# Local attention and a gated feed-forward on one core: source order on every engine in the pairs of blocks too

## The chip, the cores and the metric

The kernel runs on one core of one Trainium2 chip. The metric is the device time of one execution in microseconds (us), the median of several runs.

## The reference

```
q, k, v: (8, 8, 576, 64)   chunks of 64 rows
attn = softmax(q_c k_c^T / 8) per chunk;  out = attn v_c
x = out as (4608 tokens, 512)
h = x @ w_in (512 x 2048);  g = h * clip(h + 3, 0, 6) / 6
y = g @ w_out (2048 x 512)
```

Everything is float32. The kernel gets that precision from matmuls in fp32r: each operand is split into a high half (a cast) and a low half (the operand minus its high half), and three matmuls (high x high, high x low, low x high; L229 to L231, the helper `passes`) make one product.

## The kernel before, in words

The 4608 tokens are nine blocks of 512. Everything is transposed: a block's x and g lie with features on the 128 partitions and 512 tokens in a row. Blocks 0 to 2 are computed plainly (`mm1`, `gate`, `mm2`); beside them the attention of the next blocks runs, and the weights are converted and combined for what follows. Blocks 3 to 8 are three pairs (s = 0, 1, 2). For a pair, each of the two products of 2 x 2 blocks of matrices is done with seven products instead of eight, numbered 1 to 7, whose sums and differences are made on DVE and POOL.

A pair has 112 slots, each of six matmuls on PE. The first 56 are `first_product`: 8 columns p of 7 slots, in the order `ORDER_A` = 1, 5, 6, 7, 2, 3, 4. The products 1, 5 and 7 of a column take one of four PSUM banks `acc`, 6 one of two banks `h`; 2, 3 and 4 add on to the banks of 1, 5 and 7. What follows each product is put into a table `todo` by slot, and `tick(slot)` at the slot's end writes it out: after 1 a copy p1 (ACT, L612); after 6 the additions u2 = product 6 + p1 and u4 = product 5 + u2 (DVE, L575); after 7 the sum h = product 7 + u4; then for h, 2, 3 and 4 a ReLU on ACT (L586) and the gate on DVE (L587), for 3 and 4 with an addition of u2 before it. The gates fill tiles g0 to g3 (`gs`), each for two columns. After the gate of 3, POOL makes two differences (L595), into g and into t20 to t23.

The second 56 slots are `second_product`: in the order `ORDER_B` = 1, 5, 6, 7, 2, 4, 3, for each product 8 slots, two to an operand. The operands are made by `units`, 28 of them, four (for g0 to g3) to a product: a split, which is a cast on ACT (L423) and a subtraction on DVE (L424) into one of 8 buffers `xop`. After the split for product 5, DVE also makes a difference in g (L642); after that for product 6 (from t20 to t23), POOL makes one (L644). They are put into the table from five slots before the second product, one each 1.75 slots. The operands of the next pair's first product come from `x_operands`: seven splits, with four differences between them (L435, on POOL), put at slots 100 to 112.

Beside the first two pairs runs the attention of the next pair, four units of it, at slots 6, 23, 40 and 78: scores on PE (64 matmuls, L150), their maximum m, the difference e and then exp (L165, L169, ACT L170), the sum z and its reciprocal (L175 to L177), e times that (L179), eight transposes on PE (L188) and a copy (L190), 64 values matmuls (L200) and a copy (L211). Weights come in 1 MB tiles `ws` through SP (`fetch`, L418, three buffers), as do qk and v (L132, L142).

The order on each engine's queue is what the change is about. Up to the end of block 2 the program stands within `tc.manual_schedule()`, entered at line 281 and held by `order`: every engine runs its instructions in the order in which the source makes them. `order.close()` at line 559 ends this; from there a list scheduler of the framework orders each engine's instructions by its own estimate of when they can start, and the order of `todo` only guides it.

Of the kernel before, what the change touches and what calls it, by code (L numbers as in the profile page):

```python
# [42 lines left out]
def tile_kernel(ctx: ExitStack, tc: tile.TileContext, qk_in, v_in, weights, out):  # L43
# [236 lines left out]
    order = ExitStack()  # L280
# [275 lines left out]
        mm2(*item)  # L556
    for _ in made:
        pass
    order.close()
    std.close()  # L560
    op = pool("op2", 2)
    gs = pool("gs", 1)
# [132 lines left out]
    def tick(slot):  # L695
        for _, f in sorted(todo.pop(slot, []), key=lambda t: t[0]):
            f()
# [24 lines left out]
        second_product(s, base + SLOTS)  # L722
    for slot in sorted(todo):
        tick(slot)


# [24 lines left out]
```

## Time and profile before

| | us |
|---|---|
| median of 3 runs | 829.07 (828.84 to 829.14) |
| the profiled execution | 828.22 |
| its span | 826.4 |
| PE busy | 807.9 (98%) |
| DVE busy | 619.1 (75%) |
| ACT busy | 365.2 (44%) |
| POOL busy | 138.5 (17%) |

The first pair's first matmul starts about 328 us after the span's start, the second pair's at 497.4, the third's at 667.4. The granted TensorE clock is full throughout. Rows of a timeline give start, length, engine, line and operation, the tile written and those read, shapes, and in brackets how long the engine had been idle and what ended that. PE is the tensor engine's matmuls, PEld its weight loads, DVE the vector engine, ACT the scalar engine, POOL GpSimd, SP the queue of the DMAs. Consecutive alike instructions share a row (x4), with their time from first start to last end.

### The profile page before, as it was taken

How to read it: one execution, taken by the hardware profiler on the slowest of the kernel's cores; microseconds unless marked ns; L12 is line 12 of the kernel's file. 1: busy time of each engine (PE TensorE's matmuls, PEld its weight loads, DVE VectorE, ACT ScalarE, POOL GpSimd, SP SyncE). 2: the span in 40 equal slices, each digit the busy share in tenths (PEclk: the TensorE clock that was granted, in tenths of full speed). 3: DMA queues.
4: the chain of work that ended last, by engine and by line, in shares of the span. 5: the costliest groups of instructions: out<-in, count | busy, mean ns of one | idle time of the engine just before them, and what ended most of it. 6: DMA issues, size and time to landing. Idle time of an engine off the chain costs nothing.

```text
span 826.4 us, 13753 instructions
## 1 busy us (share of the span) xinstructions
PE 807.9 (98%) x5714; PEld 653.3 (79%) x5714; DVE 619.1 (75%) x760; ACT 365.2 (44%) x459; POOL 138.5 (17%) x79
## 2 busy tenths in 40 slices
PE   8989999999999999999999999999999999999998
PEld 5767788888877888788788887888788887878886
DVE  5888765887868864777889666777898566679951
ACT  4767752434335453433463432434644423336330
POOL 1300000000000000122262031222450212227100
PEclk9999999999999999999999999999999999999999
DMA  8982002669877971565645777567455664555573
GB/s 341 403 352 78 1 1 77 210 224 283 256 252 252 319 284 52 192 230 205 247 184 207 238 255 241 187 224 255 178 204 182 226 230 178 181 204 187 192 229 127
DMA packets 50413, 172.85 MB, mean 209 GB/s; under 512 B 4656, under 2 KB 16944, under 8 KB 39728
## 3 DMA queue, kind: packets, MB, share of 16 engines
q1 hardware_dynamic: 50352, 171.99, 59.4%
q8 instruction: 45, 0.74, 0.4%
q14 instruction: 16, 0.13, 0.0%
HBM read 133.17 MB, written 38.80 MB: 208 GB/s over the span
## 4 chain that ended last, share of the span: by engine, by line
PE 75%; DVE 14%; ACT 5%; issue 3%; DMA 1%; POOL 1%; SPq 0%; ACTq 0%; DVEq 0%; POOLq 0%
PE acc L229 16%; PE acc L230 15%; PE acc L231 15%; PE h L229 8%; PE h L230 7%; PE h L231 7%; PE two L200 2%; DVE xop L424 2%; PE two L188 2%; DVE u L107 1%; DVE g L587 1%; DVE u L575 1%; PE two L150 1%; DMA w<-w_in_out 1%; DVE e L169 1%
## 5 line engine op out<-in xcount | busy, mean ns | idle before, releaser
L229 PE MATMUL acc<-xop,ws 128*128 128x512 f32 x528 | 208.5, 396 | 4.7 <-DVE u L575 4.7
L230 PE MATMUL acc<-xop,ws 128*128 128x512 f32 x528 | 205.7, 390 | 0.0
L231 PE MATMUL acc<-xop,ws 128*128 128x512 f32 x528 | 205.3, 390 | 0.0
L229 PEld LDWEIGHTS acc<-xop,ws 128*128 128x128 f32 x528 | 99.1, 188 | 28.0 <-DVE u L575 7.1
L424 DVE TENSOR_TENSOR xop<-g,xop 128x1024 fp32r<-128x1024 f32 x72 | 103.3, 1468 | 21.5 <-ACT xop L423 21.5
L595 POOL TENSOR_TENSOR g<-g 128x512 f32<-128x512 f32 x24 | 34.7, 1446 | 500.4 <-DVE g L587 500.4
L231 PEld LDWEIGHTS acc<-xop,ws 128*128 128x128 f32 x528 | 99.1, 188 | 21.1
L230 PEld LDWEIGHTS acc<-xop,ws 128*128 128x128 f32 x528 | 99.2, 188 | 19.7
L423 ACT CAST xop<-g 128x1024 fp32r<-128x1024 f32 x72 | 74.3, 1050 | 78.8 <-PE acc L231 51.3
L229 PE MATMUL acc<-g,w 128*128 128x512 f32 x192 | 76.5, 399 | 0.5 <-ACT g L249 0.5
L229 PE MATMUL h<-x,w 128*128 128x512 f32 x188 | 75.1, 400 | 0.9 <-ACT w L112 0.9
L231 PE MATMUL h<-x,w 128*128 128x512 f32 x188 | 74.1, 394 | 1.7 <-POOL w L114 1.1
L230 PE MATMUL acc<-g,w 128*128 128x512 f32 x192 | 75.4, 393 | 0.2 <-DVE g L251 0.2
L231 PE MATMUL acc<-g,w 128*128 128x512 f32 x192 | 75.4, 393 | 0.0
L230 PE MATMUL h<-x,w 128*128 128x512 f32 x188 | 73.8, 392 | 0.0
L586 ACT ACTIVATE r<-acc,half 128x512 f32<-128x512 f32 x72 | 48.6, 686 | 26.8 <-DVE acc L575 26.0
L586 ACT ACTIVATE r<-h,half 128x512 f32<-128x512 f32 x24 | 16.5, 687 | 95.2 <-DVE h L575 95.2
L246 DVE SCALAR_TENSOR_TENSOR r<-r,h 128x512 f32<-128x512 f32 x48 | 32.7, 682 | 33.6 <-ACT r L245 33.5
L230 PE MATMUL h<-xop,ws 128*128 128x512 f32 x144 | 56.1, 390 | 0.1
L229 PE MATMUL h<-xop,ws 128*128 128x512 f32 x144 | 56.3, 391 | 0.0
L231 PE MATMUL h<-xop,ws 128*128 128x512 f32 x144 | 56.1, 389 | 0.0
L587 DVE SCALAR_TENSOR_TENSOR g<-r,acc 128x512 f32<-128x512 f32 x72 | 48.6, 682 | 7.3 <-ACT r L586 7.1
(90 smaller groups left out, 1255.4 us busy)
## 6 DMA issues: line engine op xcount, KB each, us to landing
ws<-b SPq DMA_DIRECT2D x42, 1024.0 KB, 4.8
ws<-a SPq DMA_DIRECT2D x24, 1024.0 KB, 4.9
ws<-a SPq DMA_DIRECT2D x24, 768.0 KB, 4.3
w<-w_in_out SPq DMA_DIRECT2D x16, 1024.0 KB, 14.8
qk<-qk_in SPq DMA_DIRECT2D x16, 1024.0 KB, 6.1
v<-v_in SPq DMA_DIRECT2D x17, 512.0 KB, 5.2
out_t<-o SPq DMA_DIRECT2D x32, 256.0 KB, 4.7
a<-hl SPq DMA_DIRECT2D x32, 256.0 KB, 3.3
```

The lines of the kernel that those rows point to most:

```text
L107: DVE.tensor_tensor(out=u, in0=u, in1=r, op=ALU.add)
L188: PE.transpose(out=self.tp[:, a, i], in_=self.e[:, a, 2 * i:2 * i + 2].rearrange("p c t -> p (c t)"), identity=ident)
L200: PE.matmul(self.po[o, s, a, i, :], lhsT=self.v[rows, a, i, o], rhs=self.aT[rows, a, i, o], start=True, stop=True)
L229: PE.matmul(ps, lhsT=a_h, rhs=b_h, start=first, stop=False, skip_group_check=more)
L230: PE.matmul(ps, lhsT=a_h, rhs=b_l, start=False, stop=False, skip_group_check=more)
L231: PE.matmul(ps, lhsT=a_l, rhs=b_h, start=False, stop=last, skip_group_check=more)
L246: DVE.scalar_tensor_tensor(out=r, in0=r, scalar=1.0, in1=h, op0=ALU.min, op1=ALU.mult)
L423: ACT.copy(out=t[:, :, 0], in_=src)
L424: DVE.tensor_tensor(out=t[:, :, 1], in0=src, in1=t[:, :, 0].bitcast(F32), op=ALU.subtract)
L586: return (lambda: ACT.activation(out=r, in_=ps, func=AF.Relu, bias=half, scale=1.0 / 6.0), lambda: DVE.scalar_tensor_tensor(out=out, in0=r ...
L587: lambda: DVE.scalar_tensor_tensor(out=out, in0=r, scalar=1.0, in1=ps, op0=ALU.min, op1=ALU.mult))
L595: sub = lambda o, x, y: lambda: POOL.tensor_tensor(out=o, in0=x, in1=y, op=ALU.subtract)
```

## The change

`order.close()` moves from line 559, behind block 2, to the end of the function: the pairs stand within the manual schedule as well. No instruction is added or taken out; each engine's order in the pairs becomes that of the source. From line 560 on the changed kernel's lines have numbers one lower (L586 for L587, L641 for L642); the texts use those of before.

```diff
@@ -556,7 +556,6 @@
         mm2(*item)
     for _ in made:
         pass
-    order.close()
     std.close()
     op = pool("op2", 2)
@@ -722,6 +721,7 @@
         second_product(s, base + SLOTS)
     for slot in sorted(todo):
         tick(slot)
+    order.close()
```

Three places on DVE follow, all in the first pair; the second has the same.

First, the change of columns p = 0 to p = 1, with the first attention unit beside it. Before:

```order
L587 SCALAR_TENSOR_TENSOR g0_3238<-r_3300,acc_3256 128x512
L587 SCALAR_TENSOR_TENSOR g0_3238<-r_3312,acc_3273 128x512
L165 TENSOR_REDUCE m_3363<-two_3317 128x16
L169 TENSOR_TENSOR e_3374<-two_3317,m_3363 128x1024
L175 TENSOR_REDUCE z_3441<-e_3374 128x16
L575 TENSOR_TENSOR u2_3384<-h_3377,p1_3357 128x512
```

Now:

```order
L586 SCALAR_TENSOR_TENSOR g0_3237<-r_3299,acc_3255 128x512
L574 TENSOR_TENSOR acc_3272<-acc_3272,u2_3270 128x512
L165 TENSOR_REDUCE m_3362<-two_3316 128x16
L586 SCALAR_TENSOR_TENSOR g0_3237<-r_3311,acc_3272 128x512
L169 TENSOR_TENSOR e_3373<-two_3316,m_3362 128x1024
L574 TENSOR_TENSOR u2_3383<-h_3376,p1_3356 128x512
```

The sum z has gone from ahead of u2 to seven instructions behind u4, and the addition for product 4 stands behind the gate of product 3.

Second, the last column of the first product, p = 7, around u2, u4 and h. Before:

```order
L424 TENSOR_TENSOR xop_4027<-g1_3239,xop_4027 128x2x512
L424 TENSOR_TENSOR xop_4059<-g2_3240,xop_4059 128x2x512
L575 TENSOR_TENSOR u2_4010<-h_4003,p1_3987 128x512
L642 TENSOR_TENSOR g1_3239<-t21_3243,g1_3239 128x1024
L575 TENSOR_TENSOR u4_4011<-acc_3994,u2_4010 128x512
L642 TENSOR_TENSOR g2_3240<-t22_3244,g2_3240 128x1024
L575 TENSOR_TENSOR h_4003<-acc_4015,u4_4011 128x512
```

Now:

```order
L424 TENSOR_TENSOR xop_4011<-g0_3237,xop_4011 128x2x512
L574 TENSOR_TENSOR u2_4009<-h_4002,p1_3986 128x512
L574 TENSOR_TENSOR u4_4010<-acc_3993,u2_4009 128x512
L424 TENSOR_TENSOR xop_4026<-g1_3238,xop_4026 128x2x512
L574 TENSOR_TENSOR h_4002<-acc_4014,u4_4010 128x512
L586 SCALAR_TENSOR_TENSOR g3_3240<-r_4023,h_4002 128x512
L586 SCALAR_TENSOR_TENSOR g3_3240<-r_4045,acc_3979 128x512
L424 TENSOR_TENSOR xop_4058<-g2_3239,xop_4058 128x2x512
```

The two differences L642 have left this place; the split of g0 for product 1, which with the L642 of g0 stood in columns 1 and 2 before, has come to it, and the split of g2 stands behind two gates.

Third, the operands of products 5 and 6 at the start of the second product. Before:

```order
L424 TENSOR_TENSOR xop_4121<-g3_3241,xop_4121 128x2x512
L587 SCALAR_TENSOR_TENSOR g3_3241<-r_4070,acc_4015 128x512
L642 TENSOR_TENSOR g3_3241<-t23_3245,g3_3241 128x1024
L424 TENSOR_TENSOR xop_4137<-g0_3238,xop_4137 128x2x512
L424 TENSOR_TENSOR xop_4149<-g1_3239,xop_4149 128x2x512
L424 TENSOR_TENSOR xop_4165<-g2_3240,xop_4165 128x2x512
L424 TENSOR_TENSOR xop_4185<-g3_3241,xop_4185 128x2x512
L424 TENSOR_TENSOR xop_4205<-t20_3242,xop_4205 128x2x512
```

Now:

```order
L424 TENSOR_TENSOR xop_4120<-g3_3240,xop_4120 128x2x512
L586 SCALAR_TENSOR_TENSOR g3_3240<-r_4069,acc_4014 128x512
L424 TENSOR_TENSOR xop_4136<-g0_3237,xop_4136 128x2x512
L641 TENSOR_TENSOR g0_3237<-t20_3241,g0_3237 128x1024
L424 TENSOR_TENSOR xop_4148<-g1_3238,xop_4148 128x2x512
L641 TENSOR_TENSOR g1_3238<-t21_3242,g1_3238 128x1024
L424 TENSOR_TENSOR xop_4164<-g2_3239,xop_4164 128x2x512
L641 TENSOR_TENSOR g2_3239<-t22_3243,g2_3239 128x1024
L424 TENSOR_TENSOR xop_4184<-g3_3240,xop_4184 128x2x512
L641 TENSOR_TENSOR g3_3240<-t23_3244,g3_3240 128x1024
L424 TENSOR_TENSOR xop_4204<-t20_3241,xop_4204 128x2x512
```

All four differences stand here now, each behind its own split for product 5. On POOL the first L435 has gone from ahead of the four L644 to behind them. On PE a few single matmuls of the first product move by some places, and the values matmuls of the third attention unit, which stood in three pieces in each of the two pairs that have one, are one piece. On SP the loads of qk and v have moved against those of the weights and the outputs; the first qk of a pair is now loaded when the pair begins, where it was loaded some tens of slots earlier.

## The prediction

> **What bounds the kernel now.** I read the page's busy times first, then the waits of PE from 325 us on (where the pairs begin), then the timeline around each wait.
>
> ```profile
> PE 807.9 (98%) x5714; PEld 653.3 (79%) x5714; DVE 619.1 (75%) x760; ACT 365.2 (44%) x459; POOL 138.5 (17%) x79
> PE acc L229 <- DVE u L575: 4.7, 6, 1.5
> 692.96 0.39 PE L231 MATMUL acc<-xop,ws 128*128 128x512 f32 x1
> 694.22 0.50 PE L229 MATMUL acc<-xop,ws 128*128 128x512 f32 x1 [0.87 <-DVE u L575]
> 694.56 0.39 PE L230 MATMUL acc<-xop,ws 128*128 128x512 f32 x1
> 428.56 0.39 PE L229 MATMUL acc<-xop,ws 128*128 128x512 f32 x1
> 434.00 0.39 PE L229 MATMUL acc<-xop,ws 128*128 128x512 f32 x1
> 767.54 0.39 PE L229 MATMUL h<-xop,ws 128*128 128x512 f32 x1
> 768.07 0.50 PE L230 MATMUL h<-xop,ws 128*128 128x512 f32 x1
> 768.07 0.19 PEld L230 LDWEIGHTS h<-xop,ws 128*128 128x128 f32 x1 [0.56 <-DVE xop L424]
> ```
>
> PE is the bound. Four slots (24 matmuls) go from 428.56 to 434.00, so a matmul starts every 0.227 us and a slot takes 1.36, though a row shows 0.39: an idle of PE costs its length plus 0.16. In the pairs PE has six listed waits, all for u4 (L575, which reads the bank that i=3 accumulates on): 4.7 + 6 x 0.16 = 5.7 us. After a wait the next matmul comes 0.34 later instead of 0.23 (694.22 to 694.56), 0.11 more; four of the six are such plain waits (two come right behind values matmuls, which pay it anyway): 0.4. A seventh, unlisted one stands at 768.07: PE reaches slot 72 of the third pair, whose second matmul needs the low half of the i=6 operand, 0.3 before DVE has made it (0.4 with the restart). The change can win no more than these and the pieces below; it loses wherever DVE comes later.
>
> **What goes away.**
>
> ```profile
> 345.90 0.50 PE L229 MATMUL acc<-xop,ws 128*128 128x512 f32 x1 [0.24 <-DVE u L575]
> 413.03 0.51 PE L229 MATMUL acc<-xop,ws 128*128 128x512 f32 x1 [1.15 <-DVE u L575]
> 515.47 0.50 PE L229 MATMUL acc<-xop,ws 128*128 128x512 f32 x1 [0.24 <-DVE u L575]
> 744.00 0.50 PE L229 MATMUL acc<-xop,ws 128*128 128x512 f32 x1 [0.74 <-DVE u L575]
> 342.78 0.39 PE L229 MATMUL acc<-xop,ws 128*128 128x512 f32 x1
> 343.31 1.22 DVE L175 TENSOR_REDUCE z<-e 128x16 f32<-128x1024 f32 x1 [1.12 <-ACT e L170]
> 344.44 0.68 DVE L575 TENSOR_TENSOR u<-h,p 128x512 f32<-128x512 f32 x1
> 360.58 0.39 PE L231 MATMUL acc<-xop,ws 128*128 128x512 f32 x1
> 360.89 1.16 PE L200 MATMUL two<-e,v 64*64 64x64 f32 x64
> 361.99 0.50 PE L229 MATMUL acc<-xop,ws 128*128 128x512 f32 x1
> 362.32 0.39 PE L230 MATMUL acc<-xop,ws 128*128 128x512 f32 x1
> ```
>
> The first of these (345.90, in the second pair 515.47): z stands before u2 on DVE and waits 1.12 for the exp. After the change z comes seven instructions behind u4; i=6 ends with slot 9, when slot 10 starts (342.78), so u2 can start near 343.0 and u4 ends by 344.5, while slot 12 could begin at 342.78 + 2 x 1.36 = 345.5: gone. The one at 694.22 goes with the early L642 of g0. Those at 413.03 (twin in the second pair) and 744.00 are u4 behind two L424 and an L642; they change form, below. The values matmuls (L200) of the third attention unit, in three pieces in the first two pairs, become one piece: entering costs 360.89 - 360.58 - 0.23 = 0.08, leaving about 0.1, the restart 0.1, so 0.3 each, four pieces, 1.2. All that can go: 5.7 + 0.4 + 0.4 + 1.2 = 7.7 us.
>
> **Last column of the first product (p=7), third pair.**
>
> ```profile
> 735.03 0.69 ACT L586 ACTIVATE r<-acc,half 128x512 f32<-128x512 f32 x1 [1.45 <-DVE acc L575]
> 402.38 0.39 PE L229 MATMUL acc<-xop,ws 128*128 128x512 f32 x1
> 741.97 0.39 PE L229 MATMUL acc<-xop,ws 128*128 128x512 f32 x1
> L587 DVE SCALAR_TENSOR_TENSOR g<-r,acc 128x512 f32<-128x512 f32 x72 | 48.6, 682 | 7.3 <-ACT r L586 7.1
> L423 ACT CAST xop<-g 128x1024 fp32r<-128x1024 f32 x72 | 74.3, 1050 | 78.8 <-PE acc L231 51.3
> 417.94 1.23 DVE L424 TENSOR_TENSOR xop<-g,xop 128x1024 fp32r<-128x1024 f32 x1
> 405.94 1.30 POOL L595 TENSOR_TENSOR g<-g 128x512 f32<-128x512 f32 x1 [9.23 <-DVE g L587]
> 407.19 3.45 DVE L424 TENSOR_TENSOR xop<-g,xop 128x1024 fp32r<-128x1024 f32 x2 [0.73 <-ACT xop L423]
> 401.34 1.22 DVE L179 TENSOR_TENSOR e<-e,z 128x1024 f32<-128x1024 f32 x1
> ```
>
> DVE's new order, with 0.7 for a gate, an addition or a ReLU: the ReLU of i=3 ends 735.7, gate 736.4, addition for i=4 737.05, its ReLU 737.8, gate 738.55; ACT then copies p1 and casts g0 (1.05) to 739.25, L424 of g0 (1.23) ends 740.5, u2 and u4 741.85. Slot 54, i=3, starts at 741.97: no wait. L424 of g1, now between u4 and h, ends 743.0 and h 743.6; slot 55 (i=4) wants h's bank at 743.33 and waits 0.3. The gate of i=2 ends 745.75, 0.1 late for slot 56. With restarts 0.6.
>
> In the first two pairs z also stands before the gate of i=3. First pair: slot 48 starts at 402.38, the addition for i=3 ends 403.5, z with its two small steps 405.1, the gate 405.75; so POOL's two L595 (1.30 each) begin about 405.8, and L179 falls beside the first. L424 beside an L595 took 3.45 for two where one takes 1.23. L179 never met POOL, so its price lies between 1.22 (alone) and 2.3 (the second of those L424); I take the upper, since it too reads two SBUF tiles. Then u4 ends 411.75, h 413.5, PE waits 0.35 and 0.3, with restarts 0.9 a pair; at 1.22 all comes 0.65 earlier and both waits vanish.
>
> The Trainium skill, SBUF — State Buffer, section "Who interferes with whom", says that a VectorE instruction with two SBUF inputs and a GpSimd one that reads SBUF exclude each other; L179 would then be held, and the sum would have these 0.9 twice; without the rule for L179 it is 1.8 lower. No row of L179 shows it.
>
> **Start of the second product: the large term.** The splits of the i=5 operands (L424 of g0 to g3) are needed one each two slots from slot 64, those of i=6 (L424 of t0 to t3, the tiles t20 to t23) from slot 72.
>
> ```profile
> 425.08 9.04 DVE L424 TENSOR_TENSOR xop<-g,xop 128x1024 fp32r<-128x1024 f32 x4
> 426.37 13.36 POOL L644 TENSOR_TENSOR g<-g,t 128x1024 f32<-128x1024 f32 x4 [2.30 <-DVE xop L424]
> 753.50 13.43 POOL L644 TENSOR_TENSOR g<-g,t 128x1024 f32<-128x1024 f32 x4
> 763.54 3.39 POOL L644 TENSOR_TENSOR g<-g,t 128x1024 f32<-128x1024 f32 x1
> 757.89 3.43 DVE L424 TENSOR_TENSOR xop<-g,xop 128x1024 fp32r<-128x1024 f32 x1
> 761.24 3.42 DVE L642 TENSOR_TENSOR g<-t,g 128x1024 f32<-128x1024 f32 x1
> 764.59 3.42 DVE L424 TENSOR_TENSOR xop<-t,xop 128x1024 fp32r<-128x1024 f32 x1
> ```
>
> While POOL runs L644, every L424 and L642 takes 3.42 instead of 1.23: the two engines alternate, one instruction each, 13.4 / 4 = 3.35 a round, of which DVE works 1.1 and POOL 2.25. Before, a round served one split; against PE's 2.72 for two slots DVE lost 0.6 a round and its lead just sufficed (768.07 is where it didn't). The new order puts L642 of g0 to g3 between the i=5 splits; three of them stood in the first product before. L644 of a block still waits only for the L424 of that block (it overwrites what that split reads), not for L642: the fourth L644 starts at 763.54 while L642 of the same block is still running (761.24 + 3.42). When a split ends, DVE has L642 queued and goes on; POOL gets its turn after it. So a round is split 1.1, L642 1.13, L644 2.25: 4.5 us per two slots.
>
> Third pair, continued: L424 of g2 ends 747.2; addition, ReLU, gate of i=3 749.3; L595 twice to 751.9, L424 of g3 held till then, to 753.0; gate of i=4 753.6; i=5 split of g0 754.75. Slot 56 begins near 745.1, so slot 64 at 756.2: lead 1.65 with the 0.23 of its first matmul. The four rounds end the splits of g1, g2, g3, t0 at 759.2, 763.7, 768.15, 772.65; without waits PE would want t0's at 756.2 + 8 x 1.36 + 0.23 = 767.3. The four waits (0.1, 1.6, 1.6, 1.7) with restarts add up to 5.4. The split of t1 ends 773.8, early again; from there DVE needs 1.13 against 2.72.
>
> First pair, by the same steps: h ends 413.5, the gate of i=2 415.6, L424 of g2 417.15, the gate of i=3 419.3, L595 421.9, L424 of g3 423.0, the gate of i=4 423.6, the i=5 split of g0 424.7; PE has slot 55 from 413.6, the values matmuls from 415.0, slot 56 from 416.25, slot 64 from 427.25 (lead 2.75). t0 ends 424.7 + 4 x 4.48 = 442.6. L435, now behind the L644s on POOL, then takes one more turn (2.2) before t1 ends at 445.95, wanted at 441.1: 4.9. Second pair the same, 4.9.
>
> **Other queues.** On SP the qk loads move later.
>
> ```profile
> DMA to landing us min/median/max: 4.7/6.1/13.2
> 497.42 0.39 PE L229 MATMUL acc<-xop,ws 128*128 128x512 f32 x1
> 497.19 1.28 DVE L656 TENSOR_TENSOR o<-h,u 128x512 f32<-128x512 f32 x2
> ```
>
> The tightest is the second pair's first, now behind the first output of L656: issued near 498.3, wanted by the scores behind slot 6, 497.4 + 9.6 = 507.0; 6.1 lands at 504.4: hidden, and it would cost 4.5 at the worst landing of 13.2. The v loads have over ten slots. ACT's and PE's other moves follow DVE's; the last eight DVE instructions keep their order but for one split, so the tail is unchanged.
>
> **Sum.** Waits after: 4.9 + 4.9 + 5.4 + 0.9 + 0.9 + 0.6 = 17.6; before 7.7; +9.9 us. The profiled execution took 828.22 (span 826.4 and 1.8 around it) and would come to 838.1; the median of the runs shown is 829.07, 0.85 above it, so I say 839.0.
>
> **Rivals.** Faster: the hold does not act on the new order and a round costs DVE only 1.23 + 1.13 = 2.4, under 2.72. Then 15.2 of the 17.6 vanish: 829.1 + 2.4 - 7.7 = 823.8. It decides by the round c: with the first pair's lead no wait arises for 4(c - 2.72) < 2.75, c < 3.4, and the whole breaks even near c = 3.9. For it: rounds of 3.35 caused no wait in two pairs. Against: L642 itself stands at 3.42 beside L644. Half the loss: POOL takes its turn only after L642, so that the next split slips in before L644 (L644 waiting for L642 as well). Then t0 ends 440.3, t1 443.6 in the first pair, 3.3 a pair with restarts: 834. Against it speaks 763.54. No difference: the gains and a loss of about 2.5 a pair cancel; it needs c near 3.9, between the round seen (3.35) and the one worked out (4.5).
>
> **Chances.** The forecast (834.5 to 844) 0.70, half the loss (831.5 to 835) 0.12, faster 0.12, no difference 0.06. A difference under 0.2% can't be told from none here; slower is 0.70 + 0.12 = 0.82. Of the range, 831.5 is the half case with both L179 terms gone, 843.5 the sum with the p=7 terms twice as large and L435 holding t1 in full.
>
> **What would show it.** PE waits for DVE xop L424 of 1 to 2 us at slots 68, 70, 72 and 74, where there are none now; L642 at 1.2 and L644 at about 4.5 apart; no waits near 345.9, 515.5 and 694.2; L200 in runs of 64 only; small waits on u4 and h in p=7. It is wrong if L644 stays 3.35 apart in that stretch or runs clear of the i=5 splits, or if PE waits for scores.

## The result and the profile after

The changed kernel takes 838.45 us (median; 838.17 to 839.65), the kernel before on the same chip 828.96: a ratio of 1.0118, 95% interval 1.0101 to 1.0136. 839.0 had been forecast. The profiled execution is the 839.65 one, span 837.5. 1.56 of that lies ahead of the pairs: PE waits for the first qk load of all (`L150 ... 1.6 <-DMA qk<-qk_in 1.6`), whose place the change does not touch. Lines from L560 on have numbers one lower: L641 is the DVE difference L642, L643 the POOL difference L644, L574 the additions, L586 the gates, L594 the POOL differences L595.

The busy times of the changed kernel, and the waits of PE in its pairs that the view lists, which leaves the shortest out (us in total, times, longest):

```profile
PE 809.2 (97%) x5714; PEld 651.7 (78%) x5714; DVE 621.1 (74%) x760; ACT 364.5 (44%) x459; POOL 135.3 (16%) x79
PE acc L230 <- DVE xop L424: 7.3, 7, 1.5
PE h L230 <- DVE xop L424: 5.0, 5, 1.5
PE acc L229 <- DVE u L574: 0.5, 1, 0.5
```

Busy times hardly tell the two kernels apart (PE 807.9 before, DVE 619.1). The waits do: the six for u4 with 4.7 us have become one of 0.5, and twelve for a split's low half, 12.3 us, have appeared. Where, the timeline of PE in the first pair shows. The four rows without a bracket are the first matmuls of slots 0, 64, 80 and of the next pair; the bracketed ones are the second matmuls of slots 68, 70, 72 and 74:

```profile
329.40 0.39 PE L229 MATMUL acc<-xop,ws 128*128 128x512 f32 x1
428.07 0.39 PE L229 MATMUL acc<-xop,ws 128*128 128x512 f32 x1
434.58 0.50 PE L230 MATMUL acc<-xop,ws 128*128 128x512 f32 x1 [0.68 <-DVE xop L424]
439.04 0.50 PE L230 MATMUL acc<-xop,ws 128*128 128x512 f32 x1 [1.45 <-DVE xop L424]
443.51 0.50 PE L230 MATMUL h<-xop,ws 128*128 128x512 f32 x1 [1.45 <-DVE xop L424]
446.84 0.50 PE L230 MATMUL h<-xop,ws 128*128 128x512 f32 x1 [0.32 <-DVE xop L424]
456.23 0.39 PE L229 MATMUL acc<-xop,ws 128*128 128x512 f32 x1
502.01 0.39 PE L229 MATMUL acc<-xop,ws 128*128 128x512 f32 x1
```

Such starts cut each pair into three stages. Us, first / second / third pair:

| | slots 0 to 64 | 64 to 80 | 80 to the next pair, or the end |
|---|---|---|---|
| before | 100.73 / 101.07 / 89.31 | 23.08 / 23.08 / 22.19 | 45.78 / 45.78 / 47.57 |
| changed | 98.67 / 99.00 / 87.57 | 28.16 / 28.17 / 27.47 | 45.78 / 45.78 / 47.56 |

Slots 0 to 64 gained 5.87 over the three pairs, slots 64 to 80 lost 15.45, the rest stayed: +9.57. The lossy stretch on DVE and POOL, first pair:

```profile
429.96 1.21 DVE L641 TENSOR_TENSOR g<-t,g 128x1024 f32<-128x1024 f32 x1
431.09 3.43 DVE L424 TENSOR_TENSOR xop<-g,xop 128x1024 fp32r<-128x1024 f32 x1
434.45 1.21 DVE L641 TENSOR_TENSOR g<-t,g 128x1024 f32<-128x1024 f32 x1
430.11 3.33 POOL L643 TENSOR_TENSOR g<-g,t 128x1024 f32<-128x1024 f32 x1 [1.16 <-DVE xop L424]
434.60 3.31 POOL L643 TENSOR_TENSOR g<-g,t 128x1024 f32<-128x1024 f32 x1 [1.16 <-DVE xop L424]
```

A round goes from 430.11 to 434.60, 4.49 us. L643 is released by the end of a split and begins with L641, which was queued and goes on undisturbed (1.21); L643 does its own 2.2 only then, and the next split stands from 431.09 until that is over (3.43). PE takes 2.72 for the two slots that one round serves.

One execution of a kernel below, that with L642 ahead of the i=7 splits, took 1339.3 us at a mean granted clock of 0.557; its ratio is of the others, but it is the one that was profiled, so no stages are read from that kernel.

### The profile page after: what moved, and what is told of

Its sections match the earlier page's. It is cut to its first block, busy times and chain, and to the rows that moved or that the text cites. A ratio compares the mean times of both kernels' runs of the same rounds, so it can differ in the third digit from the quotient of the medians.

```text
span 837.5 us, 13780 instructions
## 1 busy us (share of the span) xinstructions
PE 809.2 (97%) x5714; PEld 651.7 (78%) x5714; DVE 621.1 (74%) x760; ACT 364.5 (44%) x459; POOL 135.3 (16%) x79
## 4 chain that ended last, share of the span: by engine, by line
PE 71%; DVE 18%; ACT 5%; issue 4%; DMA 2%; POOL 0%; SPq 0%; DVEq 0%; ACTq 0%; POOLq 0%
PE acc L229 15%; PE acc L230 14%; PE acc L231 14%; PE h L229 7%; PE h L230 7%; PE h L231 7%; DVE xop L424 7%; PE two L200 2%; PE two L150 2%; PE two L188 2%; DVE u L107 1%; DVE g L641 1%; DMA w<-w_in_out 1%; ACT r L585 1%; DVE g L586 1%
## 5 line engine op out<-in xcount | busy, mean ns | idle before, releaser
L424 DVE TENSOR_TENSOR xop<-g,xop 128x1024 fp32r<-128x1024 f32 x72 | 107.7, 1515 | 22.7 <-ACT xop L423 22.7
L594 POOL TENSOR_TENSOR g<-g 128x512 f32<-128x512 f32 x24 | 31.0, 1294 | 501.3 <-PE two L150 297.1
L586 DVE SCALAR_TENSOR_TENSOR g<-r,acc 128x512 f32<-128x512 f32 x72 | 49.0, 681 | 30.8 <-ACT r L585 30.8
L245 ACT ACTIVATE r<-h,half 128x512 f32<-128x512 f32 x48 | 32.8, 683 | 47.9 <-PE h L231 47.9
```

The source lines that it names most:

```text
L245: ACT.activation(out=r, in_=h, func=AF.Relu, bias=half, scale=1.0 / 6.0)
L424: DVE.tensor_tensor(out=t[:, :, 1], in0=src, in1=t[:, :, 0].bitcast(F32), op=ALU.subtract)
L586: lambda: DVE.scalar_tensor_tensor(out=out, in0=r, scalar=1.0, in1=ps, op0=ALU.min, op1=ALU.mult))
L594: sub = lambda o, x, y: lambda: POOL.tensor_tensor(out=o, in0=x, in1=y, op=ALU.subtract)
```

## The experiments

All kernels were timed beside the kernel before, whose median was 828.6 to 829.5 on the chips used; ratios are to it. The same three stages are read from each, but for the one named above.

**L644 on DVE.** Is it POOL's turn that costs?

```diff
-                    POOL.tensor_tensor(out=g[pp][:, 0, 1], in0=g[pp][:, 1, 0], in1=t2[pp], op=ALU.subtract)
+                    DVE.tensor_tensor(out=g[pp][:, 0, 1], in0=g[pp][:, 1, 0], in1=t2[pp], op=ALU.subtract)
```

> The changed kernel, with L644 (difference in g from t20 to t23) made by DVE instead of POOL, at the same place of the source. POOL has nothing to do in that stretch, DVE one more instruction of 1.2 us behind each i=6 split. Theory (DVE and POOL alternate, and the turn of 2.25 that POOL takes is the loss): L424 and L642 fall to 1.13 to 1.23, a round of two is 2.4 against PE's 2.72, the i=6 rounds are also 2.4, the waits at slots 68 to 74 vanish; about 825, 823 to 827.5, although DVE has 12 x 1.2 = 14 us more work. Rival (DVE is the limit by its own work there): PE's waits for xop stay or grow, 838 to 845.

822.45 us (822.23 to 823.89), ratio 0.9928 (0.9912 to 0.9945). Page, and DVE in the first pair:

```profile
PE 805.0 (98%) x5714; PEld 652.4 (80%) x5714; DVE 607.2 (74%) x772; ACT 364.2 (44%) x459; POOL 95.7 (12%) x67
428.46 1.21 DVE L641 TENSOR_TENSOR g<-t,g 128x1024 f32<-128x1024 f32 x1
429.60 1.21 DVE L424 TENSOR_TENSOR xop<-g,xop 128x1024 fp32r<-128x1024 f32 x1
430.74 1.21 DVE L641 TENSOR_TENSOR g<-t,g 128x1024 f32<-128x1024 f32 x1
```

A round is 2.28 (428.46 to 430.74), slots 64 to 80 take 23.08 / 23.08 / 21.76, and no wait of PE is left in the pairs but five of under 0.3 in column p=7. DVE has 12 instructions more and is busy 13.9 us less: each difference on POOL had cost DVE 2.2 of waiting, and one that DVE makes itself costs it 1.13.

**The same edit in the kernel before.** Is the gain that of the source order or of L644?

> The kernel before, with only L644 moved from POOL to DVE, the order in the pairs left to the scheduler. It tells whether the 6.4 us that the changed kernel with L644 on DVE gains come from source order or from L644. Theory (from source order: z out of the way of u4, values matmuls in one piece): the six waits on u4 stay or change places, only the wait at slot 72 of the third pair (0.4) goes; 827 to 830. Rival (POOL's turns slow down DVE everywhere, their absence is the gain): 822 to 824.

828.01 (827.68 to 829.48), ratio 0.9986 (0.9977 to 0.9995). The waits of PE:

```profile
PE acc L229 <- DVE u L575: 4.4, 6, 1.2
```

All six waits for u4 are there; the third pair's 64 to 80 got shorter (21.76, before 22.19), and the second pair's 0 to 64 by 0.39. So L644 alone brings about 1. The rest of the gain is source order's: 828.01 - 822.45 = 5.6, of which 0.6 is a difference between the two kernels before that they ran beside (829.48 and 828.85); by the traces slots 0 to 64 differ by 5.8, close to the 5.87 above.

**Source order in the second product alone** (the manual schedule only around the call of `second_product`). Which half of the change loses?

> Half of the change: the scheduler orders the pairs as in the kernel before, and only what the second product writes out stands in source order. All four L642 stand behind their i=5 splits as in the changed kernel; column p=7 has the splits of g1 and g2 ahead of u2 as before, and no L642. Theory (the loss is the second product's start, the gain of about 5.9 is in the first): slots 64 to 80 take 27 to 28.5 in each pair instead of 23.1, slots 0 to 64 about 100 to 101 as before; 829 + 3 x 4.5 = about 842, 839 to 845. Rival (the loss needs the late splits of p=7 as well): within 2 of 829.

834.78 (834.53 to 835.52), ratio 1.0067 (1.0053 to 1.0081); stages 99.05 / 99.02 / 88.21 and 26.87 / 26.87 / 25.55.

```profile
PE h L230 <- DVE xop L424: 4.9, 5, 1.5
PE acc L230 <- DVE xop L424: 3.6, 3, 1.4
PE acc L229 <- DVE u L575: 2.2, 5, 0.9
```

The second product's order does lose by itself (+3.79, +3.79, +3.36), but 842 was expected, as I had forgotten what its own move gives: with L642 gone from the first product, waits for u4 fall from 4.7 to 2.2, the third unit's values matmuls come in one piece here too, and slots 0 to 64 gain 4.8. The same move of L642 pays twice, with opposite signs. The loss is 1.3 smaller than in the changed kernel in the first two pairs (1.9 in the third) because the rounds start with more lead over slot 64; in the first pair it is 426.96 - 423.18 = 3.8 where the changed kernel has 428.07 - 425.64 = 2.4 (its order in p=7 brings the first i=5 split later):

```profile
423.18 3.31 POOL L644 TENSOR_TENSOR g<-g,t 128x1024 f32<-128x1024 f32 x1 [3.58 <-DVE xop L424]
426.96 0.39 PE L229 MATMUL acc<-xop,ws 128*128 128x512 f32 x1
```

**L642 ahead of the i=7 splits.**

```diff
+                if i == 7:
+                    b = g[pp][:, 0, 0]
+                    DVE.tensor_tensor(out=b, in0=t2[pp], in1=b, op=ALU.subtract)
                 u = operand()
...
-                if i == 5:
-                    b = g[pp][:, 0, 0]
-                    DVE.tensor_tensor(out=b, in0=t2[pp], in1=b, op=ALU.subtract)
-                elif i == 6:
+                if i == 6:
```

> The changed kernel, with the four differences L642 of g0 to g3 (tt g = t - g, DVE) taken from between the i=5 splits and put one each ahead of the four i=7 splits. Same instructions, only DVE's order differs. Theory (the loss is the L642 that stands in the round with POOL's L644): the rounds of the i=5 splits fall from 4.47 us back to 3.3 to 3.4, the waits of PE for xop (7.3 on acc and 5.0 on h) shrink to under 1.5 in all, the small waits on u4 and h in column p=7 stay; time 838.5 - 12.3 - 10 x 0.16 + 1 = about 825, 823.5 to 827.5. In the third pair, where the lead at slot 64 is smallest, a wait of up to 0.5 at slot 72 may stay. Rival (DVE has too much work there, whatever the order, or the loss lies in the rest of the source order): the waits only move to the i=7 operands, and the time stays within 836 to 840.

840.9, ratio 1.0144 (1.0127 to 1.016): slower than the changed kernel, where 825 was expected. Why is taken from the run with both edits, below, which has this one too. For this kernel it is not shown, but its granted clock of 0.992 to 0.994, against 0.999 to 1.0 in the changed kernel, is like the 0.989 to 0.992 of that run.

**The two splits of p=7 moved.** Unit 0 goes from slot 51 to 45, unit 1 from 52 to 53.

```diff
-            at(base + SLOTS - 5 + int(1.75 * k), lambda k=k, unit=unit: unit(k), rank=1)
+            at(base + SLOTS + ((-11, -3)[k] if k < 2 else int(1.75 * k) - 5), lambda k=k, unit=unit: unit(k), rank=1)
```

> The changed kernel, with the split of g0 for product 1 put 6 slots earlier (out of column p=7, ahead of u2) and that of g1 behind h instead of ahead of it. Theory (the small waits of p=7 come from these two splits standing ahead of u4 and h on DVE): the waits of 0.27 and 0.24 in the first pair, 0.62 and 0.25 in the second and 0.25 in the third shrink to under 0.1 each, 1.6 + 5 x 0.16 = about -2 us in all, the large waits at slots 68 to 74 stay: about 836.3, 835.3 to 837.5. Rival (u4 and h are late because L179 is held by POOL alone, or the splits hold up something else that is waited for): waits of the same size stay or appear elsewhere in p=6 and 7, 838 to 839.

837.77 (837.66 to 839.39), ratio 1.0112 (1.0097 to 1.0127). The waits of p=7 are gone in two pairs and slots 0 to 64 take 0.75 and 1.05 less; but 64 to 80 take 29.04 and 29.01, 0.88 and 0.84 more. In the third pair a wait of 0.6 for a gate took the place of one of 0.25. PE at slot 68 and POOL's first difference, first pair:

```profile
432.98 0.50 PE L230 MATMUL acc<-xop,ws 128*128 128x512 f32 x1 [1.48 <-DVE xop L424]
424.03 3.33 POOL L643 TENSOR_TENSOR g<-g,t 128x1024 f32<-128x1024 f32 x1 [2.89 <-DVE xop L424]
```

The pair begins at 327.67, so the rounds start 96.4 in, as in the changed kernel (425.64 - 329.40 = 96.2). PE comes earlier to wait longer: 0.68 at slot 68 became 1.48.

**Both edits.**

> Both edits together: the differences L642 ahead of the i=7 splits, and the two splits moved out of the way of u4 and h in column p=7. If both causes are right and do not act on each other, all waits of PE in the pairs are gone: 838.5 - 13.9 - 2 + 0 to 1 = about 823, 822 to 825, faster than both kernels. If the lead at slot 64 gets smaller by the moved split of g1, a wait of 0.5 to 1 a pair appears at slots 64 to 72 and the time is 824 to 826.

840.74 (839.54 to 841.65), ratio 1.0143 (1.0127 to 1.0158). Slots 64 to 80 take 23.08 / 23.08 / 21.76, as the theory wants. But 80 to the next pair takes 54.53 and 54.59 instead of 45.78, and the third pair's end 49.59 instead of 47.56. ACT's cast for i=7, DVE's split, then PE in slot 88 (here L637 is L642), and the windows of that stretch (length, busy us of PE, PEld, DVE, ACT, POOL; granted clock, DMA share, GB/s):

```profile
446.17 1.23 DVE L424 TENSOR_TENSOR xop<-g,xop 128x1024 fp32r<-128x1024 f32 x1 [1.19 <-ACT xop L423]
448.64 1.05 ACT L423 CAST xop<-g 128x1024 fp32r<-128x1024 f32 x1 [2.50 <-DVE g L637]
449.73 1.23 DVE L424 TENSOR_TENSOR xop<-g,xop 128x1024 fp32r<-128x1024 f32 x1 [1.20 <-ACT xop L423]
...
463.89 0.47 PE L229 MATMUL acc<-xop,ws 128*128 128x512 f32 x1 [2.98 <-issue]
464.20 0.39 PE L230 MATMUL acc<-xop,ws 128*128 128x512 f32 x1
467.13 0.80 PE L229 MATMUL acc<-xop,ws 128*128 128x512 f32 x1 [2.32 <-DVE u L574]
468.57 0.63 PE L229 MATMUL acc<-xop,ws 128*128 128x512 f32 x1
469.00 0.63 PE L230 MATMUL acc<-xop,ws 128*128 128x512 f32 x1
...
455.00:463.00 8.00, 5.91 (x25) 4.24 (x24) 6.81 (x7) 2.94 (x3) 0.00 (x0) 1.00 0.50 158
463.00:467.00 4.00, 0.93 (x3) 0.49 (x3) 3.13 (x6) 3.78 (x4) 0.00 (x0) 0.87 0.49 209
467.00:472.50 5.50, 5.37 (x13) 4.26 (x14) 5.43 (x8) 2.00 (x3) 0.00 (x0) 0.50 0.00 0
```

The cast must wait for the difference, the split for the cast, and the next difference stands behind that split: difference, cast and split follow one another, 3.56 a round (446.17 to 449.73), and DVE idles 1.2 of each. So it comes late to u4; PE waits 3.1 and 2.5 beyond its cadence, and then runs at half the clock for 13 matmuls (0.43 instead of 0.23: 2.7 with the restart). The experiment took away one round of three steps and built another.

**L642 behind the i=6 split of its block** (`if i == 6:` in place of `if i == 5:`).

> The changed kernel, with the differences L642 of g0 to g3 on DVE each behind the i=6 split of its block instead of the i=5 split, ahead of POOL's L644 in the source. The same instructions, DVE's order alone differs. In the run that had them ahead of the i=7 splits, the 64 to 80 stretch took 23.08 us (28.16 in the changed kernel), but the cast of each i=7 operand had to wait for its L642, and PE lost 8.75 later. Here they are done 8 slots before the casts. Theory (the loss is L642 in the rounds with L644): slots 64 to 80 take 23.1 to 23.6, slots 80 to 112 the same 45.8 as in the changed kernel, the rest too; three times about 5 less than 838.4: 823 to 825. Rival (wherever L642 goes, DVE pays for it later): over 830.

828.65 (827.65 to 829.43), ratio 0.9992 (0.9983 to 1.0001). Stages 64 to 80: 24.79 / 24.75 / 22.50; 80 on: 46.86 / 46.89 / 47.55. Most of the loss is won back, but 4 us less than I expected. DVE and PE in the first pair:

```profile
435.72 3.41 DVE L641 TENSOR_TENSOR g<-t,g 128x1024 f32<-128x1024 f32 x1
439.05 3.42 DVE L424 TENSOR_TENSOR xop<-t,xop 128x1024 fp32r<-128x1024 f32 x1
442.52 0.50 PE L230 MATMUL h<-xop,ws 128*128 128x512 f32 x1 [1.39 <-DVE xop L424]
```

L642 of g0 still meets POOL's last L644 and costs 3.41 where it was meant to be alone, so the split of t1, held by L435 on POOL, comes late at slot 74. Behind that, the transposes of the unit of slot 78 wait 0.9 a pair for L179.

**L642 later still, behind the i=6 splits of the next tiles** (that of g0 behind the split of t1, of g1 behind that of t2, of g2 and g3 behind that of t3).

> The changed kernel with L644 left on POOL and the L642 moved once more: that of g0 behind the i=6 split of the second tile t21, that of g1 behind that of t22, those of g2 and g3 behind that of t23. In the run that had each behind its own i=6 split, the one of g0 still ran beside POOL's last L644 (3.41 instead of 1.21) and the split of t1 came 1.55 late at slot 74. Theory (a DVE instruction costs 2.2 more when it takes a turn beside POOL, and nothing else matters): slots 64 to 80 fall from 24.8 to 23.1 in the first two pairs and by 0.6 in the third, 828.65 - 4 = about 824.6, 823.5 to 825.7; the wait for e of L179 (1.1 a pair, slot 91) stays or grows a little. Rival (DVE pays later, as with the differences ahead of the i=7 splits): 828 or more.

828.92 (828.16 to 832.31), ratio 1.0009 (1.0 to 1.0019). 64 to 80 is clean (23.18 / 23.19 / 21.76), and the third pair as short as with L644 on DVE (156.87 and 156.98). In the first two pairs the transposes wait for L179, in all:

```profile
PE two L188 <- DVE e L179: 5.0, 2, 2.5
```

80 to the next pair takes 48.41 and 49.85 (the second with a stretch at half the clock, last section). So the rival holds where an attention unit follows, and in the third pair, which has none, DVE catches up unseen. I read it so, without a run that shows it apart: POOL's five turns put DVE some 11 us behind (an estimate, 5 x 2.2), and order only chooses who waits for that.

**A version that beats both**: L644 on DVE, and the two splits of p=7 moved. First in all pairs (unit 1 alone in the third):

> The changed kernel with L644 on DVE, and the split of g1 for product 1 behind h in column p=7, in the first two pairs also that of g0 ahead of u2. The five waits that were left (0.28, 0.25; 0.28, 0.24; 0.26 us) go away, since nothing behind them is bound by DVE any more: 1.3 with 0.1 for some of the restarts, 822.45 - 1.5 = about 821, 820.5 to 822. If DVE's work in slots 64 to 80 still sets the end there (as it took back the whole gain of the moved splits in the run that moved only them), the time stays at 822.3 to 822.6.

822.15 (821.48 to 822.93), ratio 0.9912 (0.9899 to 0.9926). The first two pairs gained 0.7 each, as expected; the third lost 1.0:

```profile
741.41 0.50 PE L229 MATMUL acc<-xop,ws 128*128 128x512 f32 x1 [1.27 <-DVE g L586]
```

There the split of g1, now behind h, stands ahead of two gates, and slot 56 needs, for its second three matmuls, the bank that the second of them reads. Then in the first two pairs alone:

> L644 on DVE, and the two splits of column p=7 moved in the first two pairs alone; the third pair as in the run that had only L644 on DVE, since with the moved split of g1 PE waited 1.4 there at 741.41 for a gate of g that the split stood ahead of. The third pair then takes 157.0 instead of 158.0 us: 822.15 - 1.0 = about 821.1, 820.3 to 821.7. If that wait has another cause than the moved split, the time stays at 822.

820.89 (820.09 to 821.27), ratio 0.991 (0.9897 to 0.9924). Of waits in the pairs one of 0.25 is left; the stages are 97.97 / 97.90 / 87.52, 23.11 / 23.11 / 21.76 and 45.78 / 45.78 / 47.55. With nothing behind it that DVE binds, the move that brought next to nothing in the changed kernel brings about 1.5.

## Why the prediction was right

**What goes away**: forecast 7.7. The waits near 345.9, 515.5 and 694.2 are gone. In the changed kernel u4 of the first of these ends in time and PE keeps its cadence into slot 12; the third unit's values matmuls are one piece:

```profile
345.34 0.69 DVE L574 TENSOR_TENSOR u<-acc,u 128x512 f32<-128x512 f32 x1
346.84 0.39 PE L231 MATMUL acc<-xop,ws 128*128 128x512 f32 x1
347.07 0.39 PE L229 MATMUL acc<-xop,ws 128*128 128x512 f32 x1
415.96 1.16 PE L200 MATMUL two<-e,v 64*64 64x64 f32 x64
```

Slots 0 to 64 gained 5.87 with the new waits of p=7 in it (next), together some 8.1 where 7.3 of the 7.7 were to come from there. Half of the excess is a wait that my list of PE's waits did not have: in the first two pairs, too, the early L642 of g0 stood ahead of u4, which ended at 356.52 in the first pair, 0.05 before slot 19 started (356.57). PE gained 0.2 there in each of these pairs.

**Column p=7**: forecast 0.9, 0.9, 0.6 with restarts. Five waits came, in the first pair at 412.65 and 414.39, 0.27 and 0.24 beyond the cadence; in the second 0.62 and 0.25, in the third 0.25 (0.3 forecast; the one before slot 56 did not come): 1.63, with five restarts of 0.11 2.2. The disputed row:

```profile
406.66 1.29 POOL L594 TENSOR_TENSOR g<-g 128x512 f32<-128x512 f32 x1 [8.30 <-DVE g L586]
407.10 1.94 DVE L179 TENSOR_TENSOR e<-e,z 128x1024 f32<-128x1024 f32 x1
408.03 2.16 POOL L594 TENSOR_TENSOR t<-g 128x512 f32<-128x512 f32 x1
```

L179 took 1.94 beside L594 where it takes 1.22 alone, near the 2.3 that I took: it is held until the first L594 ends at 407.95, 0.85 after L179 began. The Trainium skill, SBUF — State Buffer, section "Who interferes with whom", says so for a VectorE instruction with two SBUF inputs beside a GpSimd one that reads SBUF; this trace agrees, with the 0.85.

The step that failed here is the claim beside the term, that the sum would be 1.8 lower without these waits. Moving the two splits took the waits of two pairs away and PE's later waits grew by the same: while the rounds behind bind, a gain ahead of them that does not also start them earlier is worth nothing. The terms of my sum were added as if they were independent.

**The rounds**: forecast 4.5 us a round and waits of 4.9, 4.9 and 5.4 with restarts. Measured 4.47 to 4.49; 64 to 80 grew by 5.08, 5.09 and 5.28; the third pair's had the 0.4 of 768.07 in it before, so its new waits are 5.7. Of the third pair's four waits (0.1, 1.6, 1.6, 1.7) the trace has 0.3, 1.6, 1.6 and 1.6. L435 on POOL held t1 in the first two pairs (0.32 at slot 74), not in the third, which has none. L644 on DVE shows the cause: the round falls to 2.28, the loss vanishes, while the same edit in the kernel before brings only about 1.

**Rivals.** "The hold does not act" and "POOL waits for L642" both fell by one row: L643 starts at 430.11, 0.08 after a split's end, while L641 runs, and the next split is held until L643 is over. **The qk loads** are later and hidden, as forecast: no wait for scores stands in the pairs. **Sum**: +9.9 forecast, +9.57 by the stages, +9.5 by the medians. The misses are small, and in part cancel: 0.8 more went away, p=7 cost 0.2 less, the rounds 0.7 more.

## What to carry to other kernels

An engine at 75% can bind for 15 us: write down, for the stretch in question, how many of its instructions fall into one turn of the engine it shares with, and compare that round with the consumer's cadence. Moving work to a second engine that holds up the first need not be a relief: here each difference on POOL cost DVE 2.2, and on DVE 1.13. And a small wait ahead of a bound stretch is not a gain in reserve; it is worth something only once the stretch behind it no longer binds.

## What the runs showed of the hardware that I had not expected

PE's clock halved inside a kernel that keeps it 97% busy. In the run with both edits PE stood idle for 2.98, ran three matmuls and stood idle again, for 2.32 (464.81 to 467.13). The granted clock fell within that second idle: the mean of 0.87 from 463.0 to 467.0 makes 1.0 us at half the clock, so from about 466.0. It stayed at 0.50 through 472.5 (0.43 a matmul). Both pairs of that kernel that have attention beside them show it. In the run with L642 behind the i=6 splits of the next tiles, an idle of 2.49 left the clock alone in the first pair. In the second it fell to half at about 638.0, 2.0 into an idle of 2.46, and was full again from about 641.4:

```profile
468.20 1.06 PE L188 MATMUL two<-ident,e 128*128 128x128 f32 x8 [2.49 <-DVE e L179]
638.47 1.94 PE L188 MATMUL two<-ident,e 128*128 128x128 f32 x8 [2.46 <-DVE e L179]
638.40:641.00 2.60, 2.53 (x10) 2.43 (x11) 2.25 (x3) 0.56 (x1) 0.00 (x0) 0.50 0.48 178
```

The four waits of 0.3 to 1.5 of the changed kernel, one a round, never did. The Trainium skill, TensorE: Matmul & The Clock Gate, Part 1, has half the clock after an idle window of about 3.4 us that runs freely; the 0.50 agrees, but here the clock fell in idles of under 2.5, and in one of two like places not. What decides between the two places stays open. A wait of over 2 us can thus cost more than its length: without the 2.7 and 2.1 that the halved clock cost in its two pairs, the both-edits run would have ended at some 836 (an estimate, 840.74 - 4.8), below the changed kernel.
